# Attention and mixture-of-experts kernel: a gate asks for all operands of a later batch, the first w1 lies in two tiles, and two engines swap halves of a transpose's evacuation

## Chip, core and metric

The kernel runs on one core of a Trainium2 chip. The metric is the time of one execution in microseconds on the device. Where single runs were slow, the medians given here leave them out. Traces are of one profiled execution each; their spans are some 2 us shorter than the times, and a profiled execution can lie anywhere in the scatter of its kernel.

## The reference, cut to what matters

Eight batches pass through sliding-window attention (four heads with a plain window, four with a dilated one), the result is pooled to choose one expert per batch, and that expert's two-layer network is applied.

```python
batch, n_heads, seq, head_dim = (8, 8, 576, 64)     # _attn_setup: q, k, v in float32
B, S, D, E, F = (8, 576, 512, 8, 1024)              # _moe_setup
...
scores = np.where(masks[None, :, :, :], scores, -1000000000.0)   # window 32, or 32*4 with stride 4
...
pooled = x.mean(axis=1)
logits = pooled @ w_gate
e_idx = np.argmax(logits, axis=1)
...
h = np.maximum(x[mask] @ w1[e], 0.0)
out[mask] = gate_w[mask, None, None] * (h @ w2[e])
```

Two things follow. Each batch reads 2.1 MB of w1 and 2.1 MB of w2 besides 3.5 MB of q, k and v (float32, cast to bf16 on the way in; sizes in KB below are of the bf16, half of what is read: 295 KB for the Q, K or V of one head group). And w1 and w2 can only be asked for once the batch's attention is finished and its expert is known. That moment is "the gate" below.

## The kernel before

A software pipeline has four attention slots per batch. Slot `t` also runs pieces of the expert network of an earlier batch (ffn1 with w1, ffn2 with w2). All loads are issued from GpSimd in program order, because they cast. The loads of a batch are grouped: `qa` and `va` are Q/K and V of the first head group used (the plain-window group comes second), `qb` and `vb` of the other. The K of `qb` is first copied by VectorE into the tile `kx`, then transposed on TensorE.

```python
def emit_gate(b):
    ...                                   # 4 tiny matmuls (8 in the trace), max_with_indices
    e_val = nc.values_load(mi[0:1, 0:1].bitcast(I32), engines=[ET.Pool], ...)
    w1b = wp.tile([P, 4, F], BF16, name="w1b", tag="w1b")
    w2b = wp.tile([P, 8, DM], BF16, name="w2b", tag="w2b")
    s["w1"], s["w2"] = w1b, w2b
    fs = F // 2 if b == 0 else F          # batch 0: first half of F, then second half
    for f0 in range(0, F, fs):
        ...                               # three DMAs into w1b[..., f0 : f0 + fs]
    load_va(b + 2)
    load_qb(b + 2)
    load_w2(e_val, w2b)
    load_qa(b + 3)
    load_vb(b + 2)
...
def ffn1(b, fc, hf, eng):
    ...
        nc.tensor.matmul(hm, lhsT=s["w1"][:, c, :].rearrange("p (x m j) -> p x j m", x=2, j=4)
                         [:, fc // 4, fc % 4, :], rhs=s["xt"][:, c, cols], ...)
...
# before the loop: transposes of batch 1's K and Q, evacuated in two halves
dve, act = emit_T(1, a, "k", [trio(2, BF16), trio(1, BF16)])
sl[3].norm()
act(0)                                    # half 0 on ScalarE
dve1, act1 = emit_T(1, a, "q", [trio(0, BF16), trio(2, BF16)])
act1(0)
emit_gate(0)
dve(1)                                    # half 1 on VectorE
act1(1)
```

The softmax here doesn't subtract the row's maximum and nothing guards it: scores larger than these inputs give would overflow.

Of the kernel before, what the change touches and what calls it, by code (L numbers as in the profile page):

```python
# [12 lines left out]
BF16 = mybir.dt.bfloat16  # L13
# [6 lines left out]
P = 128  # L20
B = 8
# [5 lines left out]
F = 1024  # L27
# [18 lines left out]
def kernel(  # L46
# [14 lines left out]
    const = ctx.enter_context(tc.tile_pool(name="const", bufs=1))  # L61
    ldp = ctx.enter_context(tc.tile_pool(name="ld", bufs=4))
    wp = ctx.enter_context(tc.tile_pool(name="wp", bufs=3))
# [22 lines left out]
    def trio(k, dt=F32):  # L86
        return psN.tile([P, 512 if dt == F32 else 1024], dt, name=f"n{k}", tag=f"n{k}", space=PSUM)[:]

    def bank(dt=F32):
        return psM.tile([P, 512 if dt == F32 else 1024], dt, name="m", tag="M", space=PSUM)[:]  # L90
# [32 lines left out]
    def load_qk(b, g):  # L123
        for nm in ("k", "q"):
            load_1(b, g, nm)
# [19 lines left out]
    def load_qa(b):  # L145
        if b < B:
            load_tiles(b)
            load_qk(b, GO[0])

    def load_va(b):  # L150
        if b < B:
            load_v(b, GO[0])
            load_vt(b, GO[0])

    def load_qb(b):
        if b < B:
            load_qk(b, GO[1])

    def load_vb(b):
        if b < B:  # L160
            load_v(b, GO[1])
            load_vt(b, GO[1])
# [26 lines left out]
    for a in range(2):  # L189
        nc.sync.dma_start(  # L190
            out=wg_t[64 * a : 64 * a + 64, 0:2, :],
# [48 lines left out]
    def half(a):  # L240
        return slice(64 * a, 64 * a + 64)
# [9 lines left out]
    def emit_T(b, g, nm, tps=None):  # L251
        s = state(b)
        if g not in s["qk"]:
            s["qk"][g] = qkp.tile([P, 2, 2 * S], BF16, name="qk", tag="qk")
        qk = s["qk"][g][:, 0 if nm == "k" else 1, :]
        ld = loads[b][nm, g]
        tps = tps or [bank(BF16), bank(BF16)]
        ev = []
        for jh, (j0, j1) in enumerate(((0, 5), (5, 9))):
            tp = tps[jh][:, 0 : (j1 - j0) * P].rearrange("p (j n) -> p j n", n=P)  # L260
            for j in range(j0, j1):
                i = loads[b][nm, 2][:, j] if g == 0 else ld[:, 2 * j : 2 * j + 2, :]
                nc.tensor.transpose(out=tp[:, j - j0, :], in_=i.rearrange("p x d -> p (x d)"), identity=identb[:])  # L263
            o = qk.rearrange("p (n j) -> p n j", j=RH)[:, :, j0:j1]
            ev.append((o, tp.rearrange("p j n -> p n j")))

        def on_dve(x=0):
            nc.vector.tensor_copy(out=ev[x][0], in_=ev[x][1])  # L268

        def on_act(x=1):  # L270
            nc.scalar.activation(out=ev[x][0], in_=ev[x][1], func=AF.Copy)  # L271

        return on_dve, on_act
# [228 lines left out]
    def emit_gate(b):  # L502
        s = st[b]
        pooled = s["pooled"]
        lg = bank()[0:1, 0:E]
        for c in range(4):
            nc.tensor.matmul(lg, lhsT=pooled[:, c : c + 1], rhs=wg_t[:, c, :], start=(c == 0), stop=(c == 3))
        l_sb = small.tile([1, E], F32, name="l_sb", tag="l_sb")
        mx = small.tile([1, 8], F32, name="mx", tag="mx")
        mi = small.tile([1, 8], U32, name="mi", tag="mi")  # L510
        nc.vector.max_with_indices(mx[:], mi[:], lg)
        nc.vector.tensor_copy(out=l_sb[:], in_=lg)
        s["gate"] = (l_sb, mx)
        e_val = nc.values_load(mi[0:1, 0:1].bitcast(I32), engines=[ET.Pool], min_val=0, max_val=E - 1)
        w1b = wp.tile([P, 4, F], BF16, name="w1b", tag="w1b")
        w2b = wp.tile([P, 8, DM], BF16, name="w2b", tag="w2b")
        s["w1"], s["w2"] = w1b, w2b
        fs = F // 2 if b == 0 else F
        for f0 in range(0, F, fs):
            nc.gpsimd.dma_start(  # L520
                out=w1b[:, 2:4, f0 : f0 + fs],
                in_=moe_w1[ds(e_val, 1), 256:512, f0 : f0 + fs].rearrange("e (c p) f -> p (e c) f", p=P),
            )
            for a in range(2):
                nc.gpsimd.dma_start(  # L525
                    out=w1b[half(a), 0:2, f0 : f0 + fs],
                    in_=moe_w1[ds(e_val, 1), 128 * a : 128 * a + 128, f0 : f0 + fs].rearrange(
                        "e (h d) f -> d (e h) f", d=DH
                    ),
                )  # L530
        load_va(b + 2)
        load_qb(b + 2)
        load_w2(e_val, w2b)
        load_qa(b + 3)
        load_vb(b + 2)

    def load_w2(e_val, w2b):

        nc.gpsimd.dma_start(
            out=w2b[:].rearrange("p (x j) f -> p x (j f)", x=2),  # L540
            in_=moe_w2[ds(e_val, 1)].rearrange("e (x p j) f -> p (e x) (j f)", x=2, p=P),
        )

    def emit_gate_w(b):
        s = st[b]
        l_sb, mx = s["gate"]
        negm = small.tile([1, 1], F32, name="negm", tag="negm")
        nc.vector.tensor_scalar_mul(out=negm[:], in0=mx[:, 0:1], scalar1=-1.0 / S)
        esum = small.tile([1, 1], F32, name="esum", tag="esum")
        etmp = small.tile([1, E], F32, name="etmp", tag="etmp")  # L550
        nc.scalar.activation(
            out=etmp[:], in_=l_sb[:], func=AF.Exp, scale=1.0 / S, bias=negm[:], accum_out=esum[:]
        )
        nc.vector.tensor_scalar_add(out=esum[:], in0=esum[:], scalar1=1e-9)
        gw = small.tile([1, 1], F32, name="gw", tag="gw")
        nc.vector.reciprocal(out=gw[:], in_=esum[:])
        s["gw"] = gw
# [9 lines left out]
    def ffn1(b, fc, hf, eng):  # L567
        s = st[b]
        if fc == 0 and hf == 0:
            s["ht"] = htp.tile([P, 8, S], BF16, name="ht", tag="ht")  # L570
        cols = slice(HALF * hf, HALF * hf + HALF)
        hm = bank()[:, 0:HALF]
        for c in range(4):
            nc.tensor.matmul(  # L574
                hm, lhsT=s["w1"][:, c, :].rearrange("p (x m j) -> p x j m", x=2, j=4)[:, fc // 4, fc % 4, :], rhs=s["xt"][:, c, cols], start=(c == 0), stop=(c == 3)
            )
        o = s["ht"][:, fc, cols]
        if eng == "A":
            nc.scalar.activation(out=o, in_=hm, func=AF.Relu)  # L579
        else:  # L580
            nc.vector.tensor_scalar_max(out=o, in0=hm, scalar1=0.0)  # L581
# [47 lines left out]
    for b in range(B):  # L629
        for n in (0, 2):  # L630
            t = NSLOT * b + n
# [46 lines left out]
    sl = [slot(t) for t in range(len(PIECES))]  # L678


    a, z = GO
# [8 lines left out]
    dve, act = emit_T(0, z, "k", [trio(0, BF16), trio(1, BF16)])  # L690
# [8 lines left out]
    dve, act = emit_T(0, z, "q")  # L699
# [21 lines left out]
    sl[3].ln()  # L721
    sl[3].rd()
    dve, act = emit_T(1, a, "k", [trio(2, BF16), trio(1, BF16)])
    sl[3].norm()
    act(0)
    dve1, act1 = emit_T(1, a, "q", [trio(0, BF16), trio(2, BF16)])
    act1(0)
    emit_gate(0)
    dve(1)
    act1(1)  # L730
    emit_pair(1, "k")
    emit_pair(1, "q")
    sl[4].sx()
    dve, act = emit_T(1, z, "k")
    sl[4].mask()
    act(1)
    dve(0)
    sl[5].sx()
    sl[4].av_a()
    dve, act = emit_T(1, z, "q")  # L740
    sl[4].av_b()
    dve(0)
    act(1)
    sl[5].mask()
    sl[4].ln()
    sl[4].rd()
    sl[6].sx()
# [4 lines left out]
    sl[5].rd()  # L752
    sl[6].mask()
    sl[5].norm()
    emit_gate_w(0)


    def piece(b, x, e):
# [8 lines left out]
    for t in range(7, len(PIECES)):  # L767
        cur, pre = sl[t], sl[t - 1]
        n = PIECES[t]

        lead = n >= 5 and done % 21 < 16 and pre.on
        items = []
        for i, x in enumerate(range(done, done + n)):
            e = "A" if (lead and i == 0) or 2 * i >= n else "D"
            items.append(lambda x=x, e=e: piece(x // 21, x % 21, e))
        done += n
        gb, gn = divmod(t - 5, NSLOT)
        if gn == 0 and 0 < gb < B:
            emit_gate(gb)
        if t > 7:  # L780
            run_T(t)
        pre.av_a()
        flush()
        if gn == 2 and gb < B:
            emit_gate_bc(gb)
        cur.sx()
        if pre.on and not cur.on:
            items.pop(0)()
            n -= 1
        pre.av_b()  # L790
        if lead:
            items.pop(0)()
            n -= 1
        pre.ln()
        cur.mask()
        pre.rd()
        if t == 7:
            run_T(t - 1)
            run_T(t)
        k0 = n // 2  # L800
        for f in items[:k0]:
            f()
        pre.norm()
        for b, g, nm in tsched.get(t + 1, []):
            if g == 0:
                emit_pair(b, nm)
        for f in items[k0:]:
            f()
        if gn == 1 and 0 < gb < B:
            emit_gate_w(gb)  # L810
    flush()

# [29 lines left out]
```

## Time and profile before

| | before |
|---|---|
| time, median of 4 runs at first | 217.78 us (217.46 to 218.15) |
| span of the profiled execution | 214.7 us (its own time 216.45, on the fast side) |
| TensorE, VectorE, ScalarE busy | 90%, 60%, 63% |
| HBM read / written | 62.41 / 9.44 MB |

The page's chain that ended last, by line, shows which transfers it runs through: the DMA's 36% are loads, in the first 132 us, and TensorE has 47%.

```profile
PE 47%; DMA 36%; issue 5%; ACT 4%; POOL 3%; DVE 3%; POOLq 1%; SPq 0%
DMA qm<-in_q_dram 19%; PE m L574 18%; PE m L594 15%; DMA w2b<-in_moe_w_dram 7%; DMA w1b<-in_moe_w_dram 7%; DMA km<-in_k_dram 4%; PE n L347 4%; PE m L263 3%; PE m L609 2%; PE ps L284 2%; ACT qk L271 1%; PE m L347 1%; POOL w1b L525 1%; ACT rd L457 1%; ACT pt L317 1%
```

### The profile page before, as it was taken

Reading aid. Unit: us, or ns where it says so; the run is one execution under the profiler, and the core shown is the slowest. Engines: PE = TensorE matmul, PEld = TensorE weight load, DVE = VectorE, ACT = ScalarE, POOL = GpSimd, SP = SyncE. Lnnn points to the kernel's source line nnn. Section 1 sums busy time; section 2 is a strip of 40 time slices with the busy share of each in tenths; the row PEclk is TensorE's granted clock in tenths of the full one; section 3 lists DMA queues with packets and bytes.
Section 4 is the critical chain, followed back from the end, with each engine's and each line's share of the span. In section 5 each row is a group of like instructions: output and inputs, shape, how many; then the busy total and the mean of one; then the engine's idle time right before and its main releaser. Section 6 shows DMA issues by size and latency. Waiting matters only on the chain.

```text
span 214.7 us, 7448 instructions
## 1 busy us (share of the span) xinstructions
PE 193.9 (90%) x3145; PEld 140.6 (65%) x3145; DVE 129.3 (60%) x358; ACT 136.0 (63%) x271; POOL 84.6 (39%) x133
## 2 busy tenths in 40 slices
PE   5867675899989999999999995999999999999991
PEld 1645554777558965886588753896588557748741
DVE  5665566676677756875677564775777465425312
ACT  2577775777658876788658861987678755332320
POOL 7986195507451286127531456148404000400000
PEclk9965575799999999999999999999999999999999
DMA  5999989999999999999999999999999994399323
GB/s 74 186 186 196 149 106 178 213 202 107 195 234 242 219 204 216 246 246 199 203 251 250 200 200 250 223 221 206 217 231 188 211 212 165 58 208 225 123 102 118
DMA packets 46976, 41.12 MB, mean 192 GB/s; under 512 B 24928, under 2 KB 35168, under 8 KB 46944
## 3 DMA queue, kind: packets, MB, share of 16 engines
q0 software_dynamic: 39344, 31.20, 94.8%
q1 hardware_dynamic: 7600, 9.46, 13.9%
q8 instruction: 24, 0.39, 0.7%
q14 instruction: 8, 0.07, 0.1%
HBM read 62.41 MB, written 9.44 MB: 335 GB/s over the span
## 4 chain that ended last, share of the span: by engine, by line
PE 47%; DMA 36%; issue 5%; ACT 4%; POOL 3%; DVE 3%; POOLq 1%; SPq 0%
DMA qm<-in_q_dram 19%; PE m L574 18%; PE m L594 15%; DMA w2b<-in_moe_w_dram 7%; DMA w1b<-in_moe_w_dram 7%; DMA km<-in_k_dram 4%; PE n L347 4%; PE m L263 3%; PE m L609 2%; PE ps L284 2%; ACT qk L271 1%; PE m L347 1%; POOL w1b L525 1%; ACT rd L457 1%; ACT pt L317 1%
## 5 line engine op out<-in xcount | busy, mean ns | idle before, releaser
L574 PE MATMUL m<-xt,w1b 128*128 128x288 bf16 x512 | 66.8, 288 | 1.5 <-DMA w1b<-in_moe_w_dram 1.1
L574 PEld LDWEIGHTS <-w1b 128*128 128x128 bf16 x512 | 56.8, 114 | 7.6 <-DMA w1b<-in_moe_w_dram 1.3
L594 PE MATMUL m<-w2b,ht 128*128 128x512 bf16 x256 | 57.8, 379 | 0.0
L579 ACT ACTIVATE ht<-m 128x288 bf16<-128x288 f32 x77 | 31.6, 411 | 20.5 <-PE m L574 16.8
L594 PEld LDWEIGHTS <-ht 128*128 128x128 bf16 x256 | 24.1, 98 | 27.6
L484 DVE SCALAR_TENSOR_TENSOR xt<-n,rd 128x320 bf16<-128x320 f32 (+1 forms) x58 | 29.4, 544 | 9.0 <-ACT rd L457 9.0
L324 DVE TENSOR_TENSOR pt<-pt,mk 128x896 bf16<-128x896 bf16 x32 | 20.0, 624 | 23.0 <-ACT pt L317 23.0
L271 ACT ACTIVATE qk<-m 128x512 bf16<-128x512 bf16 x28 | 20.5, 735 | 19.6 <-PE m L263 19.3
L317 ACT ACTIVATE pt<-ps 128x896 bf16<-128x896 f32 x32 | 29.0, 907 | 2.7 <-PE ps L284 2.7
L520 POOL DMA_DIRECT2D w1b<-in_moe_w_dram x9 | 6.4, 710 | 61.3 <-PE n L347 21.0
L131 POOL DMA_DIRECT2D vm<-in_v_dram x32 | 24.0, 760 | 11.1 <-DMA km<-in_k_dram 3.5
L268 DVE COPY qk<-m 128x640 bf16<-128x640 bf16 x28 | 22.8, 814 | 7.1 <-PE m L263 6.9
L581 DVE TENSOR_SCALAR ht<-m 128x288 bf16<-128x288 f32 x51 | 22.6, 454 | 5.1 <-PE m L574 4.2
L601 DVE TENSOR_SCALAR osb<-m,gbc 128x512 f32<-128x512 f32 x16 | 12.0, 749 | 17.7 <-PE m L594 17.7
L457 ACT ACTIVATE rd<-lnd 128x576 f32<-128x576 f32 x32 | 21.9, 684 | 1.0
L347 PE MATMUL n<-pt,vm 64*64 64x64 bf16 (+2 forms) x816 | 18.8, 197 | 3.0 <-DVE pt L324 2.7
L347 PEld LDWEIGHTS <-vm 64*64 64x64 bf16 x896 | 14.6, 113 | 10.3 <-issue 5.6
L451 ACT ACTIVATE lnd<-n 128x256 f32<-128x256 f32 (+1 forms) x58 | 20.4, 405 | 0.5 <-PE n L347 0.5
L347 PE MATMUL n<-pt,ones 64*64 64x128 bf16 (+3 forms) x262 | 17.2, 248 | 0.0
L284 PE MATMUL ps<-qk 64*64 64x96 bf16 (+3 forms) x608 | 14.5, 209 | 2.6 <-ACT qk L271 1.3
L284 PEld LDWEIGHTS <-qk 64*64 64x64 bf16 x608 | 14.0, 115 | 4.0 <-DVE qk L268 2.3
L599 ACT ACTIVATE osb<-m,gbc 128x512 f32<-128x512 f32 x16 | 10.9, 682 | 8.7 <-PE m L594 8.7
(71 smaller groups left out, 199.1 us busy)
## 6 DMA issues: line engine op xcount, KB each, us to landing
w2b<-in_moe_w_dram POOLq DMA_DIRECT2D x8, 1024.0 KB, 14.4
out_dram<-osb SPq DMA_DIRECT2D x32, 256.0 KB, 7.5
km<-in_k_dram POOLq DMA_DIRECT2D x16, 288.0 KB, 8.4
qm<-in_q_dram POOLq DMA_DIRECT2D x16, 288.0 KB, 9.9
w1b<-in_moe_w_dram POOLq DMA_DIRECT2D x16, 256.0 KB, 6.9
w1b<-in_moe_w_dram POOLq DMA_DIRECT2D x7, 512.0 KB, 7.4
vm<-in_v_dram POOLq DMA_DIRECT2D x8, 256.0 KB, 7.4
vm<-in_v_dram POOLq DMA_DIRECT2D x32, 64.0 KB, 14.3
```

The source lines that it names most:

```text
L131: nc.gpsimd.dma_start(out=t[:, h], in_=v[b, h, 0:512, :].rearrange("(c p) d -> p c d", p=P))
L268: nc.vector.tensor_copy(out=ev[x][0], in_=ev[x][1])
L271: nc.scalar.activation(out=ev[x][0], in_=ev[x][1], func=AF.Copy)
L284: nc.tensor.matmul(ps[half(e), a, o : o + rhs.free_size()], lhsT=lhsT, rhs=rhs, start=True, stop=True, skip_group_check=True)
L317: nc.scalar.activation(out=pt[:], in_=s["ps"][:, :, 0:NP], func=AF.Exp, scale=0.125)
L347: x = nc.tensor.matmul(oo, lhsT=lhsT, rhs=rhs, start=start, stop=True, skip_group_check=True)
L457: nc.scalar.activation(out=rd[:], in_=s["lnd", n][:], func=AF.Exp, scale=-1.0)
L484: nc.vector.scalar_tensor_tensor(out=o, in0=a0, scalar=1.0, in1=a1, op0=ALU.mult, op1=ALU.mult, accum_out=s["pool"][:, w, c : c + 1],)
L574: nc.tensor.matmul(hm, lhsT=s["w1"][:, c, :].rearrange("p (x m j) -> p x j m", x=2, j=4)[:, fc // 4, fc % 4, :], rhs=s["xt"][:, c, cols], ...
L579: nc.scalar.activation(out=o, in_=hm, func=AF.Relu)
L581: nc.vector.tensor_scalar_max(out=o, in0=hm, scalar1=0.0)
L594: nc.tensor.matmul(om, lhsT=s["ht"][:, fc, r * P : (r + 1) * P], rhs=s["w2"][:, fc, :], start=(fc == 0), stop=(fc == 7))
```

## The change

Its intent: (1) let the first expert matmuls start when the first half of w1 is there, (2) use idle time of VectorE and relieve ScalarE in the start-up, (3) move small gate-weight operations of batch 0 out of the start-up's way, (4) ask for operands of attention a whole batch earlier.

```diff
-        w1b = wp.tile([P, 4, F], BF16, name="w1b", tag="w1b")
         w2b = wp.tile([P, 8, DM], BF16, name="w2b", tag="w2b")
...
+        if b == 0:
+            w1 = [const.tile([P, 4, F // 2], BF16, name=f"w1h{x}") for x in range(2)]
+            s["w1"] = w1
+            parts = [(w1[x], F // 2 * x, F // 2) for x in range(2)]
+        else:
+            w1b = wp.tile([P, 4, F], BF16, name="w1b", tag="w1b")
+            s["w1"] = [w1b[:, :, F // 2 * x : F // 2 * x + F // 2] for x in range(2)]
+            parts = [(w1b, 0, F)]
...
-        load_va(b + 2)
-        load_qb(b + 2)
-        load_w2(e_val, w2b)
-        load_qa(b + 3)
-        load_vb(b + 2)
+        if b == 0:
+            load_va(2)
+            load_qb(2)
+            load_w2(e_val, w2b)
+            load_qa(3)
+            load_vb(2)
+        else:
+            load_vb(b + 2)
+            load_w2(e_val, w2b)
+            load_qa(b + 3)
+        load_va(b + 3)
+        load_qb(b + 3)
...
     dve, act = emit_T(1, a, "k", [trio(2, BF16), trio(1, BF16)])
+    dve(0)
     sl[3].norm()
-    act(0)
+    act(1)
...                                # at one more transpose the halves change engines the other way; sl[5].mask() ahead of sl[4].av_b()
-    emit_gate_w(0)
...
-        if gn == 2 and gb < B:
+        if (t == 8) if gb == 0 else gn == 2 and gb < B:
             emit_gate_bc(gb)
...
-        if gn == 1 and 0 < gb < B:
+        if (t == 7) if gb == 0 else gn == 1 and gb < B:
             emit_gate_w(gb)
```

More of the change, by code (lines that the diff above doesn't have):

```diff
@@ L514, in emit_gate @@
         e_val = nc.values_load(mi[0:1, 0:1].bitcast(I32), engines=[ET.Pool], min_val=0, max_val=E - 1)
-        w1b = wp.tile([P, 4, F], BF16, name="w1b", tag="w1b")
         w2b = wp.tile([P, 8, DM], BF16, name="w2b", tag="w2b")
-        s["w1"], s["w2"] = w1b, w2b
-        fs = F // 2 if b == 0 else F
-        for f0 in range(0, F, fs):
+        if b == 0:
[6 more added lines that the diff above has]
+            parts = [(w1b, 0, F)]
+        s["w2"] = w2b
+        for t, f0, fs in parts:
             nc.gpsimd.dma_start(
-                out=w1b[:, 2:4, f0 : f0 + fs],
+                out=t[:, 2:4, :],
                 in_=moe_w1[ds(e_val, 1), 256:512, f0 : f0 + fs].rearrange("e (c p) f -> p (e c) f", p=P),
@@ L525, in emit_gate @@
                 nc.gpsimd.dma_start(
-                    out=w1b[half(a), 0:2, f0 : f0 + fs],
+                    out=t[half(a), 0:2, :],
                     in_=moe_w1[ds(e_val, 1), 128 * a : 128 * a + 128, f0 : f0 + fs].rearrange(
@@ L574, in ffn1 @@
             nc.tensor.matmul(
-                hm, lhsT=s["w1"][:, c, :].rearrange("p (x m j) -> p x j m", x=2, j=4)[:, fc // 4, fc % 4, :], rhs=s["xt"][:, c, cols], start=(c == 0), stop=(c == 3)
+                hm, lhsT=s["w1"][fc // 4][:, c, :].rearrange("p (m j) -> p j m", j=4)[:, fc % 4, :], rhs=s["xt"][:, c, cols], start=(c == 0), stop=(c == 3)
             )
@@ L728 @@
     emit_gate(0)
-    dve(1)
     act1(1)
@@ L735 @@
     sl[4].mask()
-    act(1)
-    dve(0)
+    act(0)
+    dve(1)
     sl[5].sx()
@@ L740 @@
     dve, act = emit_T(1, z, "q")
-    sl[4].av_b()
+    sl[5].mask()
     dve(0)
     act(1)
-    sl[5].mask()
+    sl[4].av_b()
     sl[4].ln()
```

## The prediction

> **What bounds the kernel now.** I read the page first, then the chain that ended last, the waits of TensorE, the timeline of TensorE, VectorE and GpSimd, the busy times by stretch, and last the time to landing of every load. The page names two candidates, TensorE and the loads:
>
> ```profile
> PE 193.9 (90%) x3145; PEld 140.6 (65%) x3145; DVE 129.3 (60%) x358; ACT 136.0 (63%) x271; POOL 84.6 (39%) x133
> ...
> PEclk9965575799999999999999999999999999999999
> DMA  5999989999999999999999999999999994399323
> ...
> q0 software_dynamic: 39344, 31.20, 94.8%
> ```
>
> The DMA digits hardly leave 9 before slice 34, and queue 0, which carries all loads, fills 94.8% of the span. TensorE's clock digits are low in slices 2 to 7 (11 to 43 us) only. So there are three stages: a start-up of latencies, a middle where TensorE and loads both run full, and a tail (after some 165 us) without load pressure. The busy times by stretch show how close the two are:
>
> ```profile
> 50.00:52.00 2.00, 2.00 (x17) 1.63 (x16) 1.44 (x3) 1.93 (x6) 2.00 (x4) 1.00 0.34 30
> ...
> 64.00:87.00 23.00, 23.00 (x428) 17.16 (x429) 15.94 (x44) 17.02 (x35) 10.11 (x15) 1.00 1.25 222
> 87.00:110.00 23.00, 23.00 (x438) 17.21 (x430) 15.93 (x44) 17.28 (x36) 10.13 (x15) 1.00 1.26 227
> 110.00:133.00 23.00, 21.03 (x331) 15.36 (x319) 13.68 (x41) 16.07 (x34) 9.50 (x15) 1.00 1.26 225
> ```
>
> After the length come the busy times of PE, PEld, DVE, ACT and POOL, then granted clock, DMA share and GB/s. From 64 to 110 us TensorE never stops while the DMA moves 222 to 227 GB/s; from 110 to 133 it loses 2 us. The gate matmul of a batch recurs at 69.18, 91.59 and 114.10 us: TensorE needs 22.4 to 22.5 us per batch. The last V load of a gate's set lands at 51.21, 77.34, 99.58, 123.22 and 145.79 us: the later sets take 22.2, 23.6 and 22.6 us. Loads and compute are balanced, the loads a little slower.
>
> The waits that matter are few. From the timeline:
>
> ```profile
> 34.87 0.43 PE L574 MATMUL m<-xt,w1b 128*128 128x288 bf16 x1
> ...
> 36.36 0.88 PE L574 MATMUL m<-xt,w1b 128*128 128x288 bf16 x3 [1.06 <-DMA w1b<-in_moe_w_dram]
> ...
> 63.64 0.68 PE L263 MATMUL m<-identb,kx 128*128 128x128 bf16 x9 [0.97 <-DVE kx L248]
> ...
> 132.59 0.46 DVE L248 COPY kx<-km 128x1152 bf16<-128x1152 bf16 x1 [2.70 <-DMA km<-in_k_dram]
> ...
> 133.11 0.45 PE L263 MATMUL m<-identb,kx 128*128 128x128 bf16 x5 [2.08 <-DVE kx L248]
> ```
>
> (1) The first expert matmul runs its first step at 34.87 and stalls 1.06 us for w1. (2) At 133.11 TensorE has waited 2.08 us for a K load, plus 0.20 inside the nine transposes. (3) The 0.97 us at 63.64 is no load wait: in the timeline VectorE is busy with the normalisation until 63.12 and then copies kx; the load had landed at 62.08. No part of this change touches it.
>
> **What the skill says.** "DMA: Bandwidth & Descriptors", section "Two DMAs through the same engine are not ordered": descriptors of one queue start in order but are pipelined. The trace agrees as far as order goes: queue 0's loads land in the order of issue, so I treat it as first in, first out. Section "Issuing engines are not separate DMA queues": all DMAs share the same 16 engines and interleave. It agrees: two 256 KB stores issued at 126.18 and 126.62 needed 7.6 and 10.2 us beside the loads. "TensorE: Matmul & The Clock Gate", "Part 1: The HAM clock gate": the clock is half or full, and full comes after about 3.4 us of busy array. The stretches show 0.50 (34 to 36 us) and 1.00 (40 to 42).
>
> **Part 1, w1 of batch 0 in two tiles.** The six w1 DMAs of gate 0 land at 30.93, 31.60, 33.34 (first half of F) and 34.97, 35.60, 36.22 (second). TensorE's first step went at 34.87; its second waited for 36.22, the second half, though it reads the first. The second half's region overlaps it only when taken as one range; two tiles end that. All of the first half is there at 33.34, so the 1.06 us goes. Bytes and issue count stay.
>
> **Part 2, T halves swapped.** For batch 1's first K the 640-column half goes from ScalarE to VectorE, ahead of the normalisation. VectorE idles 1.70 us there waiting for ScalarE's rd at 22.60; the copy (about 0.8 us) can start once five transposes are through, about 21.75, and fits. TensorE's 0.56 us wait at 23.30 for ScalarE's evacuation shrinks, and the copy of 0.70 us that stood after the gate leaves VectorE (24.63), so slot 4's scores, which waited 1.21 us until 25.38, can start about 0.65 us earlier. The gate itself depends on the normalisation and moves 0.1 us. The later swaps mostly fill idle time: 0.
>
> **Part 3, gate weight of batch 0 moved later.** Its etmp (0.30 + 0.18 us on ScalarE, 1.33 us idle before it) held the exponential of slot 7 to 35.37, though its scores were done at about 34.7. That frees roughly 0.7 us on ScalarE. With parts 1 and 2, ffn1 of batch 0, which resumed at 39.68, should resume 1 to 2 us earlier. How much depends on the clock window that opened at about 40 us. I take **1.5 us** by slot 8.
>
> **Part 4, the request order.** Each gate asked for w1(b), first-group V and second-group Q/K of b+2, w2(b), Q/K of b+3, last V of b+2. After: w1(b), last V of b+2, w2(b), then all of b+3 but that V. Total bytes are equal; 885 KB (591 Q/K, 295 V) move from gate 1 to gate 0 and likewise for every later gate. Two effects:
> - The queue ran dry between gates 0 and 1 (30 GB/s from 50 to 52 us). After 51.21 the first w1 piece took 4.1 us to land, against 2.1 to 2.9 at the next gates: a hole of 1.6 us, which the extra request fills.
> - Requests shift against each other. Per batch, with landings of before:
>  - K for kx: landed 0.4 us early, 0.3 early, 2.1 late, 1.5 early against its transpose less 0.54 us of copy. It is now asked for four slots (22 us) earlier: this **2.28 us** wait goes.
>  - w1(b) now stands behind the next batch's 885 KB. That block took 5.5, 6.1, 6.1, 4.9 us; less the hole's 1.6. Its slack was 5.3, 5.5, 6.8, 6.6 us (landings 82.27, 104.52, 128.20, 150.81; ffn1 at 87.55, 110.06, 134.98, 157.38). It falls to 1.4, 1.1, 2.3, 3.2.
>  - K of the first group now stands behind one V set (2.4, 2.2, 1.9, 2.1 us), less 1.6. Its slack was 1.9, 2.0, 1.7, 3.3 (landings 73.07, 95.42, 118.25, 141.56; transposes 74.97, 97.39, 119.90, 144.81). It falls to 1.1, 1.4, 1.4, 2.7.
>
> These slacks are against the old clock of TensorE: they are the most it can be ahead there. So the 1.5 us from the start is cut to about 1.1 by 110 us. Then 2.28 is saved at 131, making 3.3, and the loads of batches 4 and 7 cut it to 2.3, and to about **2.0**, because stores then also come earlier and take some of the same DMA time. After 165 us loads are no limit, and the 2.0 stays: 217.7 - 2.0 = **215.7 us**.
>
> **Rivals.**
> - A: TensorE is the only bound, and the loads keep up. Then 1.06 + about 1 + 2.28 are all kept, 4.3 us: 213.4 us, on the edge of 2%. For it: TensorE never stops from 64 to 110 us. Against: the sets' 22.2 to 23.6 us against 22.45, and slacks of 0.3 us already.
> - B: the loads are the whole bound. The wait then moves from kx to w1 and first-group K, and little more than part of the hole is gained: 217 us. For it: the chain of waits is mostly loads up to 132 us. Against: the last set before 165 us ends 1.6 us sooner too, and its w2 then lands with 2 us to spare.
> - C: the later gate-weight broadcast is late. It was issued at 35.85 and took 7.2 us; now it goes out at about 43, lands near 50, and the first ffn2 eviction needs it at about 51.5. If it takes 10 us or more, PSUM banks block TensorE for a us or two: about 217.
> - D: the clock. A shifted busy pattern at 33 to 40 us may warm one window earlier or later, about 1 us either way.
>
> **Range and chances.** The base of 215.7 with B and C on one side and A on the other gives **213.6 to 217.6**. Faster by over 2% needs under 213.4, so nearly all of A: 0.08. Slower by over 2% needs 222, for which nothing here is large enough: 0.03. Within 2%: 0.89.
>
> **What would show it.** Right: no stall for w1 near 35 us, ffn1 of batch 0 resuming near 38; no dry stretch near 51 us; no kx wait on a K load near 131; in its place short TensorE waits (0.3 to 1.5 us) at ffn1 or at first-group K, on w1 or km loads, between 75 and 145 us; 0.97 near 63 still there. Wrong: no such load waits at all (A), a wait on VectorE or ScalarE for gbc near 52 us (C), or a set time far from 22.2 to 23.6 us, which would undo every slack above.

## The result, and the profile after

| | before | after |
|---|---|---|
| median of 4 runs | 217.78 us | 214.86 us (214.32 to 215.33) |
| ratio, 95% interval | | 0.9864 (0.9836 to 0.9893) |
| span of the profiled execution | 214.7 us | 213.4 us |

A ratio is the mean time of one kernel's fast runs over that of the other's fast runs of the same rounds, so it is not quite the ratio of the medians. The two profiled executions differ by 1.3 us only: that of before was a fast one of its kernel (216.45 us), that of after the slowest of its four (215.33). The traces show where the gain comes from, the times how large it is.

The page of the changed kernel, lines that answer to those of before:

```profile
PE 191.6 (90%) x3130; PEld 139.2 (65%) x3145; DVE 130.2 (61%) x358; ACT 136.1 (64%) x271; POOL 84.5 (40%) x133
...
PEclk9965576999999999999999999999999999999999
DMA  5999979999999999999999999999999994499323
...
q0 software_dynamic: 39344, 31.20, 95.9%
...
PE 52%; DMA 35%; issue 4%; POOL 3%; DVE 2%; ACT 1%; POOLq 1%; SPq 0%
```

TensorE's 2.3 us less of busy time is no saving of work: 15 matmul records are missing (3130 of 3145). What is real is the clock line, full from slice 7 on (counted from 0) instead of slice 8. The busy times by stretch (columns as in the prediction) show more. First 33 to 40 us of the kernel before, then of the changed one:

```profile
33.00:36.50 3.50, 1.91 (x64) 1.50 (x65) 2.15 (x9) 1.90 (x5) 1.82 (x3) 0.50 1.27 187
36.50:40.00 3.50, 3.09 (x24) 2.54 (x23) 2.07 (x3) 2.69 (x6) 2.24 (x3) 0.53 1.30 208
```

```profile
33.00:36.50 3.50, 3.40 (x80) 2.97 (x81) 2.18 (x6) 2.09 (x5) 2.36 (x5) 0.56 1.20 173
36.50:40.00 3.50, 2.79 (x27) 2.40 (x24) 2.73 (x7) 2.52 (x6) 1.47 (x3) 1.00 1.34 204
```

From 36.5 to 40 us the granted clock is 1.00 instead of 0.53: in the 3.5 us ahead of it TensorE was busy for 3.40 us instead of 1.91. Then the middle of the changed kernel:

```profile
50.00:52.00 2.00, 1.95 (x14) 1.03 (x14) 1.43 (x5) 0.83 (x3) 1.73 (x3) 1.00 1.58 167
...
64.00:87.00 23.00, 22.68 (x404) 16.80 (x405) 15.86 (x43) 16.43 (x35) 10.58 (x16) 1.00 1.30 217
87.00:110.00 23.00, 22.89 (x407) 17.00 (x397) 15.72 (x43) 17.28 (x36) 10.19 (x16) 1.00 1.25 224
110.00:133.00 23.00, 21.54 (x360) 15.76 (x362) 15.30 (x43) 15.85 (x34) 9.74 (x15) 1.00 1.25 224
```

From 50 to 52 us the DMA moves 167 GB/s instead of 30: the dry stretch is gone. From 110 to 133 us TensorE still loses time. The timeline of TensorE tells on what:

```profile
34.43 1.15 PE L588 MATMUL m<-xt,w1h 128*128 128x288 bf16 x4
...
62.16 0.68 PE L263 MATMUL m<-identb,kx 128*128 128x128 bf16 x9 [0.98 <-DVE kx L248]
...
74.49 0.68 PE L263 MATMUL m<-identb,km 128*128 128x128 bf16 x9 [0.20 <-DMA km<-in_k_dram]
...
120.92 0.68 PE L263 MATMUL m<-identb,km 128*128 128x128 bf16 x9 [1.35 <-DMA km<-in_k_dram]
...
132.01 0.68 PE L263 MATMUL m<-identb,kx 128*128 128x128 bf16 x9
```

All four steps of the first ffn1 group run without a stall at 34.43. The wait for K at the kx transposes near 131 us is gone. In its place stands a wait of 1.35 us for the other group's K at 120.92, which was asked for at gate 3 and landed at 120.88 (issued 107.42, 13.46 us to landing). The 0.98 us at 62.16, VectorE's, is where it was.

How far the changed kernel is ahead of the one before can be read at each gate's first matmul (from the timelines; gate 0 to 7, us): -0.4, 1.5, 0.9, 0.5, 0.5, 1.5, 1.3, 1.3, and 1.3 at the end. The start gains 1.5. Of this 0.6 go in a pause within attention matmuls just ahead of ffn1 of batch 1 (0.43 us at 64.02, which the profile puts down to issue). Its w1 had landed shortly before, at 63.82, but that it was the cause is not shown, and in after_again and after_third the lead does not shrink there. Another 0.4 go ahead of the K at 74.49. The saved wait at 131 less the new one at 121 brings about 1.0; then little changes.

### The profile page after: what moved, and what is told of

Same layout as the page of the kernel before. It is cut to its first block, busy times and chain, and to the rows that moved or that the text cites. A ratio compares the mean times of both kernels' runs of the same rounds, so it can differ in the third digit from the quotient of the medians.

```text
span 213.4 us, 7437 instructions
## 1 busy us (share of the span) xinstructions
PE 191.6 (90%) x3130; PEld 139.2 (65%) x3145; DVE 130.2 (61%) x358; ACT 136.1 (64%) x271; POOL 84.5 (40%) x133
## 4 chain that ended last, share of the span: by engine, by line
PE 52%; DMA 35%; issue 4%; POOL 3%; DVE 2%; ACT 1%; POOLq 1%; SPq 0%
PE m L608 20%; PE m L588 17%; DMA km<-in_k_dram 12%; DMA w1b<-in_moe_w_dram 10%; DMA qm<-in_q_dram 9%; PE n L347 5%; PE m L263 4%; DMA w1h<-in_moe_w_dram 3%; PE m L623 3%; PE ps L284 2%; PE m L347 1%; PE n L263 1%; PE m L507 1%; POOL km L118 1%; POOL km L121 0%
## 5 line engine op out<-in xcount | busy, mean ns | idle before, releaser
L608 PE MATMUL m<-w2b,ht 128*128 128x512 bf16 x241 | 56.9, 379 | 0.9 <-issue 0.2
L588 PE MATMUL m<-xt,w1b 128*128 128x288 bf16 x448 | 57.5, 287 | 0.0
L588 PEld LDWEIGHTS <-w1b 128*128 128x128 bf16 x448 | 49.7, 114 | 4.9 <-issue 0.2
L271 ACT ACTIVATE qk<-m 128x512 bf16<-128x512 bf16 (+1 forms) x28 | 20.5, 737 | 19.6 <-PE m L263 19.6
L268 DVE COPY qk<-m 128x640 bf16<-128x640 bf16 (+1 forms) x28 | 22.6, 809 | 7.1 <-PE m L263 7.1
L527 POOL DMA_DIRECT2D w1b<-in_moe_w_dram x7 | 5.0, 718 | 35.6 <-DVE ht L595 18.1
(75 smaller groups left out, 213.2 us busy)
```

The source lines that it names most:

```text
L268: nc.vector.tensor_copy(out=ev[x][0], in_=ev[x][1])
L271: nc.scalar.activation(out=ev[x][0], in_=ev[x][1], func=AF.Copy)
L588: nc.tensor.matmul(hm, lhsT=s["w1"][fc // 4][:, c, :].rearrange("p (m j) -> p j m", j=4)[:, fc % 4, :], rhs=s["xt"][:, c, cols], start=(c ...
L608: nc.tensor.matmul(om, lhsT=s["ht"][:, fc, r * P : (r + 1) * P], rhs=s["w2"][:, fc, :], start=(fc == 0), stop=(fc == 7))
```

## The experiments

Theory: the loads pace the middle, and what counts is when each lands against its use. Rival A: TensorE alone is the bound. Rival B: the loads' total is the whole bound, so that the end moves only when a dry stretch of the DMA is filled. Twelve runs were made, in three groups on one chip each (four rows of the table to a group), with five rounds. The medians of the kernel before in these groups were 216.56, 217.25 and 217.18 us, with single runs from 215.77 to 219.25.

| run | median us | ratio to before | 95% interval | span of its trace, us |
|---|---|---|---|---|
| order_only | 215.11 | 0.9939 | 0.9885 to 0.9993 | 213.4 |
| start_only | 214.97 | 0.9916 | 0.9863 to 0.9968 | 213.2 |
| two_tiles | 215.80 | 0.9951 | 0.9901 to 1.0000 | 213.3 |
| after_again | 215.27 | 0.9927 | 0.9883 to 0.9971 | 213.0 |
| before_w2_once | 214.68 | 0.9878 | 0.9830 to 0.9926 | 213.4 |
| after_w2_once | 212.91 | 0.9822 | 0.9768 to 0.9877 | 210.6 |
| va_early | 213.35 | 0.9823 | 0.9771 to 0.9874 | 213.9 (slow) |
| qk_first | 217.1 | 1.0029 | 0.9969 to 1.0090 | 213.0 |
| swaps_only | 217.05 | 0.9978 | 0.9928 to 1.0027 | 216.8 |
| after_third | 215.11 | 0.9887 | 0.9846 to 0.9929 | 213.4 |
| va_early_again | 213.82 | 0.9817 | 0.9772 to 0.9862 | 212.1 |
| start_va_early | 215.43 | 0.9912 | 0.9866 to 0.9957 | 212.5 |

The ratio of qk_first leaves out only the run of 220.78 us; without the other slow run, 219.10, it is about 1.001.

### The parts alone

**order_only**: the kernel before with the change's five lines of request order and nothing else.

> The kernel before with only the request order of the change (885 KB asked for one gate earlier, last V ahead of w2). Theory (the loads pace the middle, and what counts is when each load lands against its use): the dry stretch near 51 us is filled and the wait for K at the kx copy near 131 us (2.3 us) goes, so about 2.0 us less than before, ratio 0.99; the profile shows no dry stretch. Rival A (TensorE alone is the bound): 2.3 us less, nearly the same. Rival B (loads alone are the bound): only the hole, 0.5 to 1.6 us less.

The mean saved 0.6%, the medians 1.5 us, less than the 2.0 expected but within the interval. Its trace has no wait of TensorE for a load after 42 us; the waits of TensorE in that stretch are only these:

```profile
PE m L263 <- DVE kx L248: 1.3, 1, 1.3
PE m L507 <- ACT ht L586: 0.5, 1, 0.5
PE m L601 <- issue: 0.2, 1, 0.2
```

The one kx wait is VectorE's, near 63 us. The 1.0 us stall for w1 at 36.47 is there, as it must be. This execution warmed its clock late (0.69 granted from 40 to 44 us, where the kernel before had 1.00) and was 1.0 to 1.4 us behind the trace of before up to gate 4; then it gained 2.5 us where the kernel before waits for K, and ended 1.3 us ahead.

**start_only**: the changed kernel with the old five lines of request order.

> The changed kernel with the old request order: two w1 tiles, swapped halves and later gate weight alone. Theory: ffn1 of batch 0 resumes about 1.9 us earlier as in the changed kernel, but the K loads of the kx copy had only 0.3 to 0.4 us to spare, so all but some 0.3 us of it is given back as waits for K between 85 and 131 us: ratio 0.997 to 1.0. Rival A: the 1.5 to 1.9 us is kept, ratio 0.992.

This expectation failed. 0.8% was kept, 1.6 us of the medians, and its trace is ahead by 1.3, 1.1, 1.1, 1.2, 1.5 us at gates 1 to 5 and 1.5 at the end. The wait for K near 131 us is still there, 1.74 us after 2.08:

```profile
131.60 0.45 PE L263 MATMUL m<-identb,kx 128*128 128x128 bf16 x5 [1.74 <-DVE kx L248]
```

What I had missed: when TensorE is earlier at gate 1, so are gate 1's requests. They fall into the dry stretch, which the busy times of this run show at 141 GB/s instead of 30:

```profile
50.00:52.00 2.00, 1.95 (x12) 1.01 (x11) 1.63 (x5) 0.98 (x2) 2.00 (x4) 1.00 1.00 141
```

So later loads land earlier as well (w1 of batch 2 complete at 80.75 instead of 82.27 us), and their slack against TensorE does not shrink.

**two_tiles**: the kernel before with only the two w1 tiles of batch 0 and the matching index in `ffn1`.

> The kernel before with only the first w1 in two tiles. Theory: the 1.06 us stall near 35 us is gone in the trace, but the time stays within 0.3 us of before, as the loads take the gain back. Rival A: 1.0 to 1.5 us less, ratio 0.994.

The stall near 35 us is gone. The mean saved 0.5%, nearer to Rival A's 0.994 than to the theory's 0.3 us; but the interval reaches 1.0, so that whether the gain is kept or given back is not decided by the times. In the trace it is 0.7 us ahead at gate 1, 0.3 to 0.4 at gates 2 to 4, and 1.4 from gate 5 on, where it waited 1.1 us for K instead of 2.1.

**swaps_only**: the kernel before with only the swapped halves, the mask ahead of `av_b` and the later gate weight.

> The kernel before with only the swapped halves and the later gate weight of batch 0. Theory: the scores of slot 4 come 0.6 us earlier, the exponential of slot 7 about 0.7 us earlier, but the first ffn1 still waits for the whole of w1 (36.2 us), now longer. ffn1 of batch 0 resumes at best 0.7 to 1.2 us earlier; what reaches the end is at most that, 0 to 1.2 us less than before, ratio 0.995 to 1.0.

The ratio is 0.998, no measurable gain. As expected, its ffn1 waits longer for w1: 2.1 us in the trace, whose execution was the slowest of its six (218.72 us).

**after_again** and **after_third**: the changed kernel, run again beside the others.

> The changed kernel again, as the reference for the three others of the same chip: 2.9 us less than before as at first, ratio 0.986. If the order and the start gave their gains independently (rival A), the savings of order_only and start_only add up to this; under the theory start_only alone is worth little and the two together are worth more than the sum.

> The changed kernel beside the next one on the same chip: 1.3 to 2.9 us less than before, as in the two comparisons so far.

The gain was 0.7% and 1.1% here after 1.4% at first. The savings of order_only and start_only, 0.6% and 0.8%, would add up to 1.5%; the changed kernel of the same group saved 0.7% (0.3 to 1.2). The traces end 1.3, 1.5 and 1.3 to 1.7 us ahead for order alone, start alone and both. That looks as if the parts overlap, and both do fill the same dry stretch. But it is not shown: the trace of order_only started 1.0 us behind for its clock, and in the first comparison the changed kernel saved as much as the sum of the parts.

### Taking the pressure of the loads away

**before_w2_once** and **after_w2_once**: every batch uses batch 0's w2, loaded once. Their outputs are wrong, which doesn't matter for the times. Only 14.7 MB of loads are missing.

```diff
-        w2b = wp.tile([P, 8, DM], BF16, name="w2b", tag="w2b")
+        w2b = wp.tile([P, 8, DM], BF16, name="w2b", tag="w2b") if b == 0 else st[0]["w2"]
...
     def load_w2(e_val, w2b):
+        if w2b is loaded_w2[0]:
+            return
+        loaded_w2[0] = w2b
```

> The kernel before, but every batch uses batch 0's w2, which is loaded once (wrong result on purpose): 7 of the 8 w2 loads, 14.7 of 62.4 MB read, are gone, all instructions of the compute engines stay. If the loads pace the middle, the wait for K near 131 us goes and nothing replaces it: 2.3 us less than before (ratio 0.989), no TensorE wait for a load after 42 us. If TensorE alone were the bound: the same 2.3 us at most.

> The changed kernel with w2 loaded once (wrong result on purpose). If the loads are what cut the gain of the change (all four kernels so far end 1.3 to 1.7 us ahead in their traces, whichever part they have), then without their pressure the whole start gain of 1.5 to 1.9 us and the 2.3 us of the K wait are both there: 3.8 to 4.2 us less than before, ratio 0.981 to 0.983, and 1.5 to 1.9 us less than before_w2_once. If the start gain is worth only 1.3 to 1.7 us for another reason, then the difference from before_w2_once is well under 1.5 us.

Both came out. The kernel before saved 2.6 us of the medians (2.3 expected), and no wait of TensorE for a load is left in its trace after 42 us:

```profile
PE m L263 <- DVE kx L248: 1.0, 1, 1.0
PE m L509 <- ACT ht L584: 0.5, 1, 0.5
PE m L599 <- issue: 0.2, 1, 0.2
```

The changed kernel saved 4.3 us (3.8 to 4.2 expected). The difference of the two is 1.8 us of the medians (1.5 to 1.9 expected), 1.4 of the means of six runs each; their intervals against the kernel before overlap. In the trace after_w2_once is 2.0 us ahead at gate 1, about 1.5 at gates 2 to 4, and 4.1 from gate 5 on. Only these waits of TensorE are left in it after 42 us:

```profile
PE m L263 <- DVE kx L248: 1.0, 1, 1.0
PE m L509 <- ACT ht L598: 0.5, 1, 0.5
PE m L593 <- DMA w1b<-in_moe_w_dram: 0.4, 1, 0.4
PE m L613 <- issue: 0.2, 1, 0.2
```

So the two parts of the change are worth about 4 us to TensorE, as Rival A's sum said, and it is the loads that take part of it back. That holds with the same instructions on every compute engine: in the traces the changed kernel waits 1.6 to 2.0 us for K loads after 42 us with all loads, and 0.4 us for w1 without w2's.

### Filling the other dry stretch

**va_early** and **va_early_again**: the changed kernel with one request moved ahead of gate 0.

```diff
     load_qk(2, GO[0])
+    load_va(2)
...
         if b == 0:
-            load_va(2)
             load_qb(2)
```

> The changed kernel with batch 2's first V (295 KB) requested before gate 0 instead of after it, so that it fills the other dry stretch, 26 to 28 us. If the middle is paced by the loads, each us of dry stretch filled is a us at the end: 1.3 to 1.8 us less than the changed kernel (ratio to before about 0.985 on this chip), provided the first w1 half still lands by 34.4 us. If TensorE is the bound, at most the load waits left in its trace (about 1.5 to 2 us), of which this removes part.

> The changed kernel with batch 2's first V ahead of gate 0, again, now beside the changed kernel itself. If a filled dry stretch of the loads is worth its length at the end: 1.0 to 1.8 us less than after_third, ratio to before 0.980 to 0.985. If the first comparison was a matter of chip and day: within 0.5 us of after_third.

The busy times from 26 to 28 us, of the changed kernel and then of va_early_again, show the stretch filled (23 and 139 GB/s):

```profile
26.00:28.00 2.00, 1.90 (x48) 1.33 (x46) 1.26 (x2) 1.93 (x3) 1.45 (x3) 0.50 0.13 23
```

```profile
26.00:28.00 2.00, 1.90 (x48) 1.41 (x45) 1.26 (x2) 1.93 (x3) 1.37 (x3) 0.50 1.09 139
```

The first half of w1 landed at 33.48 us, still in time. On the same chip the median is 213.82 us beside 215.11 for the changed kernel, 1.3 us less, and the trace is 1.3 us shorter too (212.1 and 213.4). The first comparison had the same ratio, 0.982. Its profiled execution, 215.88 us, was slow. This version beats both kernels, by 3.4 us of the medians against the one before.

**start_va_early**: the same request moved, with the old request order and parts 1 to 3.

> Parts 1 to 3 of the change with the OLD request order, and batch 2's first V ahead of gate 0. Theory: the later dry stretch (50 to 52 us) stays partly open, the earlier one is filled; the set of gate 0 ends 1.3 us sooner, K for kx comes at most as much earlier as TensorE, so about the time of start_only to 1.3 us less than that: ratio to before 0.985 to 0.992. If the new order is what matters, it stays above va_early_again by 1 us or more.

Its ratio is 0.991, at the upper end of what was expected, and 1.6 us of the medians above va_early_again: once the first dry stretch is filled the new order is worth something again. And with the old order the early V shows no gain in the times: start_only, without it, had 0.992 in its own group. Its trace, the fastest execution of its six, still waits 1.9 us for the K of kx, which the new order removes.

### Order within a set

**qk_first**: from gate 1 on, w2 and the first group's Q/K ahead of the last V.

```diff
-            load_vb(b + 2)
             load_w2(e_val, w2b)
             load_qa(b + 3)
+            load_vb(b + 2)
```

> The changed kernel with w2 and the Q and K of the first group ahead of the last V in a gate's set, so that this K, which TensorE waited for at 74 and 121 us in the changed kernel, lands about 2 us earlier. If the order within a set is what costs, 1.0 to 1.6 us less than the changed kernel. If the total of the loads paces it, the wait moves on to w1, which is not earlier, and the time stays within 0.5 us.

Neither expectation held: of the fast runs, 214.91 to 217.84 us, the median is about 2 us above that of the changed kernel (of different groups). Two further runs, 219.10 and 220.78, were slow. The trace is of the fastest run. In it the waits for the first group's K are gone and waits for w1 stand there instead, 1.6 us in all:

```profile
PE m L588 <- DMA w1b<-in_moe_w_dram: 1.6, 2, 0.9
```

That is the second expectation's mechanism, but why other fast executions took up to 2.9 us more was not seen in any trace and stays open.

### How the end follows the loads

The last load of gate 5's set is the last of the dense stream. Its landing (issue plus time to landing) and the span of the same trace:

| trace | last load of gate 5 lands | span | difference |
|---|---|---|---|
| before | 165.69 | 214.7 | 49.0 |
| after | 164.13 | 213.4 | 49.3 |
| order_only | 164.37 | 213.4 | 49.0 |
| start_only | 164.50 | 213.2 | 48.7 |
| va_early_again | 162.64 | 212.1 | 49.5 |
| swaps_only | 167.59 | 216.8 | 49.2 |
| qk_first | 165.30 | 213.0 | 47.7 |
| after_w2_once | 148.31 | 210.6 | 62.3 |

With all loads, the difference is 48.7 to 49.5 us in all but one of these kernels (48.3 in two_tiles, which is not listed); with w2 gone the two come apart. This is a correlation, and it does not say that the loads set the end: gate 5 asks for these loads, and from its first matmul TensorE needs 75.7 us to the end in before, order_only, start_only and after_w2_once alike, and 75.8 to 76.3 in the changed kernel's traces. In order_only no load holds TensorE after 42 us at all. So the loads set the pace only where TensorE runs into them: at the one K in the kernel before, and at first-group K in the changed kernel, which is ahead. What shows this are w2_once, where the waits and the lost time go together, and va_early_again, where the waits for K fall to 0.3 us (besides one of 1.1 for w1) and the lead by gate 4 is 1.6 us instead of 0.5 to 0.9.

## Why the prediction was right or wrong

The time, 214.86 us, lay in the range of 213.6 to 217.6 and 0.8 us below the 215.7; "within 2%" was right. By its steps:

- **w1 in two tiles.** Right. The second half's region held back the first: with two tiles the four steps run at 34.43 us, and the 1.06 us stall is gone.
- **Swaps.** Right in the start-up: VectorE's copy fits ahead of the normalisation (22.27 to 23.09 us), and slot 4's scores start at 24.94 instead of 25.38. Alone with the later gate weight they bring nothing measurable at the end (0.998, 0.993 to 1.003), as w1 holds ffn1 anyway.
- **Gate weight, and the sum of 1.5 us by slot 8.** The exponential of slot 7 starts at 34.23 instead of 35.37, ffn1 resumes at 37.76 instead of 39.68 (1.9 us; 1 to 2 was said). At gate 1 the lead is 1.48 us.
- **Dry stretch and kx wait.** Both gone, as said.
- **The cuts.** The form was right: short waits for first-group K, at 74 and 121 us. The sizes were less so: by gate 4 (114 us) the lead was cut to 0.5 us, not 1.1 (0.9 in after_again, 0.6 in after_third). The hole's credit was right: w1 of batches 2 to 4 was complete 3.7, 4.4 and 4.4 us later than before, where the block less 1.6 gives 3.9, 4.5 and 4.5. The term that was mis-sized is the last V set, now ahead of w2. It was counted with the 2.4, 2.2 and 1.9 us that it took at the end of its set; behind w1 it took 3.1, 3.2 and 2.9 (from the last landing of w1 to that of V). At 121 us K moreover landed 3.2 us after w2; before, it was 2.1. So first-group K landed 1.4, 1.5 and 2.6 us later instead of 0.8, 0.6 and 0.3. Stores were under way in both, so why these took longer is not seen. The list also left out w1 of batch 1, which came 5.6 us later (63.82 instead of 58.20): its own block took 7.2 us in the kernel before. (The 591 KB should be 590; the sum of 885 stands.)
- **"They are the most it can be ahead there."** This step was wrong in its reasoning. The slacks were taken from landings of before, as if loads did not move when TensorE does. An earlier gate asks earlier, and while the queue has a gap, everything behind it lands earlier. start_only shows it: 0.8% kept where this step would have left 0.3 us.
- **The final 2.0 us.** The trace says 1.3; the medians say 2.9, 1.3 and 2.1 us in three comparisons. The mechanism was right, and the scatter of the times is as large as the error. Part of the closeness is luck, as two errors work against each other: after the wait at 121 us TensorE was 1.0 us behind the kernel before instead of 1.1 ahead, but after 131 it lost only 0.2 us (0.7 in after_again, 0.6 in after_third) instead of 1.3.
- **Rivals.** A's 4.3 us is what TensorE could have (after_w2_once: 4.3), but not with the loads. B was right in that waits moved to first-group K, but 2.9, 1.3 and 2.1 us were gained, not the 0.7 of its 217. C did not happen: the broadcast went out at 42.23 us and took 6.1, and no wait for it shows. D did: the clock came up one window earlier, at about 36.5 instead of 40 us.

## What to carry to other kernels

Where loads and compute are balanced, count the us in which the DMA queue is empty, first of all those ahead of a value that decides what to load next, and give each of them something that could have been asked for anyway. It need not pay by itself: here the early V gained 1.3 us with the new order and nothing that the times show with the old one. Two changes that fill the same empty stretch need not add up. And a slack that is read from a trace holds only as long as the requests do not move with the engine that they are measured against.

## What the Trainium skill lacked or had wrong

- "DMA: Bandwidth & Descriptors" says that DMAs of all issuing engines interleave on the same 16 engines; this agrees (a store of 256 KB took 2.0 us from issue to landing in the empty tail, 5.6 to 11 beside loads). It gives no figure for a mixed stream of casting loads and stores: one batch of 7.73 MB read and 1.18 MB written took 22.24 us here, 401 GB/s, in the kernel before (77.34 to 99.58 us).
- No page says how many loads may be under way from GpSimd in a program like this one. In the kernel before, a load's issue stood until the eighth load ahead of it had landed: w1 issues at 73.36 and 75.18 us followed landings at 73.07 and 74.90, and no load of any of the traces was issued sooner than that. The runs do not show what sets the eight.
- "TensorE: Matmul & The Clock Gate", Part 1, says that half or full clock depends on a busy window of about 3.4 us. It agrees (0.56 in 33 to 36.5 us, then 1.00, with 3.40 of 3.50 us busy ahead), and what the page calls run-variable is worth 1 us or more in the start-up here: order_only, with the start-up code of the kernel before, was granted 0.69 from 40 to 44 us instead of 1.00 and was 1.0 us behind its trace at gate 1.
- No page gives the scatter to expect of a kernel that its loads pace: the kernel before took 215.77 to 219.25 us over three groups, so that 0.5% needed more than five rounds.
